# Fewer dummy matmuls ahead of the first transposes and ahead of the first FFN step of a fused attention and SwiGLU kernel

## The chip, the cores and the metric

The kernel runs on one core of a Trainium2 chip. The metric is the device time of one launch in microseconds; it was 333.8 us before the change (median of ten runs).

## What is computed

Sliding-window causal attention (8 batches, 8 heads, 576 positions, head dimension 64, window 64) is followed by a SwiGLU block over the 4608 resulting tokens (512 wide, hidden width 1536). Inputs and output are float32; the kernel works in bfloat16 with float32 accumulation.

```python
scores = scale * np.matmul(q, k.transpose(0, 1, 3, 2))
mask = (rel >= 0) & (rel < window)          # window = 64, rel = query - key
scores = np.where(mask, scores, -1000000000.0)
...                                          # softmax over keys
attn_out = np.matmul(attn, v)
x = attn_out.transpose(0, 2, 1, 3).reshape(B * S, H * D)
g = x @ w_gate
silu = g * (1.0 / (1.0 + np.exp(-g)))
val = x @ w_val
return (silu * val) @ w_out
```

## The kernel before

The tokens are cut into 36 tiles of 128 for the attention, and into 9 chunks of 512 (four tiles each) for the FFN. One list of operations is written down in program order; a small graph class finds from the buffers that each one reads and writes which semaphores it has to wait for, and every engine then runs its own operations in the order of that list. Nothing is reordered later, so the text of the list sets the order on each engine.

The list begins with two strings. `LOADS` issues the loads, nearly all on GpSimd's queue (the first tile's k and q go out on SyncE's and ScalarE's queues as float32, line 291). `STEPS` (from line 166) is the order of the work for tiles 0 to 15 and FFN chunks 0 and 1, by hand, one token for each step; from chunk 2 on a loop in `build` issues the rest. The tokens that matter here:

- `warm:50` (line 348): 50 matmuls of 64 columns over a zeroed tile `wz`, at the very start. `W:n` (`fill`, line 359): n dummy matmuls of 512 columns over `wz`, into the PSUM bank that has been free for longest. Nobody reads what they write. They wait for `wz` alone.
- `B` (line 403): a matmul that writes the mask's bias into a bank ahead of the scores. `ca`, `cd`: the cast of the first tile's q and k to bfloat16, one half on ScalarE (line 300) and one on VectorE (line 302), after their load. `T:0:1`, `T:0:0` (line 310): the transposes of those halves on TensorE; `ea`, `ed` copy the results to `kT` and `qT`.
- `TQ`, `TK` (line 310) transpose q and k of later tiles, and `qa`, `kd` and the like copy them out. `S` (line 423) are the scores with their exponentials (line 433), `M` the mask product (line 439), `A0` and `A1` (line 473) the product with v in two phases, `N` the normalisation on VectorE (lines 492 and 495), which writes `xb`; `X` (line 570) the transposes of `xb`, and `xa`, `xd` their copies to `xT`.
- `F:c:f` (line 604): for FFN chunk c and hidden block f, four matmuls with the gate weights and four with the value weights, then tanh on ScalarE (line 610). `U` (lines 613 and 615): the two VectorE steps that make the hidden block. `O` (line 637): the output projection. `ld`, `wo`: further loads.

So TensorE's order at the start is: 50 small dummies, two `B` matmuls, ten dummies, eight transposes of tile 0, four of q of tile 1, one dummy, the scores of tile 0, and so on, up to the fourth `X` and the first `F`.

Of the kernel before, what the change touches and what calls it, by code (L numbers as in the profile page):

```python
# [7 lines left out]
B, H, S, D = 8, 8, 576, 64  # L8
DM, DFF = H * D, 1536
T = B * S  # L10
# [139 lines left out]
class _Kernel:  # L150
# [13 lines left out]
    w:5:6 v:7 kq:6 w:0:1 kq:7 w:10:12  # L164
    """
    STEPS = """
    warm:50 ld:8 wo:0:6 B:0 ca:0:0 cd:0:1 W:10 T:0:1 T:0:0 ea:0:1 ed:0:0 TQ:1 qa:1 W:1 S:0 TK:1 ld:9 kd:1 W:1
    TQ:2 qa:2 S:1 B:2 TK:2 kd:2 A0:0 A1:0 M:1 S:2 TQ:3 N:0 B:3 TK:3 qa:3 kd:3 W:1 X:0 A0:1 xa:0 S:3 A1:1 ld:10
    A0:2 N:1 A1:2 ld:11 W:1 A0:3 N:2 A1:3 X:1 xa:1 N:3 W:1 X:2 xa:2 W:3 X:3 F:0:7:0:384 xd:3 U F:0:8 U TK:5
    TQ:5 ka:5 TQ:4 F:0:7:384:512 TK:4 ld:12 qa:4 qd:5 ka:4 U W:2 F:0:3 U S:4 S:5 F:0:6 M:4 F:0:4 M:5 U F:0:1 U  # L170
    U A0:4 A0:5 A1:4 ld:13 wo:6:12 A1:5 F:0:9 N:4 N:5 X:4 F:0:2 U xa:4 X:5 U F:0:5 xd:5 F:1:1:0:128 U TQ:6
    F:1:2:0:256 U TK:6 ld:14 qa:6 F:1:3:0:256 U F:0:0 kd:6 U U S:6 TK:7 TQ:7 F:1:0:0:256 kd:7 F:0:10 M:6 U
# [612 lines left out]
```

## Time and profile before

| | before |
|---|---|
| median of ten runs | 333.8 us (333.0 to 334.82) |
| profiled execution | 333.93 us, span 332.1 us |
| TensorE busy | 325.9 us (98%) |
| VectorE, ScalarE, GpSimd busy | 217.0, 137.3, 115.8 us |
| TensorE from 0 to 18.8 us, from 18.8 to 72 us | first FFN matmul at 19.03; 53.14 of 53.20 us busy |
| chain that ended last | TensorE 95%, VectorE 3% |
| `fill` (line 359) on that chain | 1% of the span |

Times in the profile are counted from the start of the span, which is 1.83 us shorter than the execution's own time. Matmuls are pipelined: a row of the timeline with ten matmuls has the length from the start of the first to the end of the last, and the end of a matmul is about 0.16 us after its last column has gone in when the array runs fast. Weight loads (PEld) are rows of their own and run ahead of the matmuls that use them. "[idle before <-releaser]" is the time for which the engine had nothing to run before that row, and what ended it.

### The profile page before, as it was taken

What the parts mean: (1) busy time and instruction counts of PE and PEld (TensorE: products, weight loads), DVE (VectorE), ACT (ScalarE), POOL (GpSimd) and SP (SyncE); (2) the same over time, 40 slices, a digit from 0 to 9 for tenths busy, and PEclk for the clock granted to TensorE, in tenths of its full rate; (3) what the DMA queues carried; (4) which work ended last, traced back from release to release, by engine and by line L of the source; (5) the groups of instructions that cost most, each with busy time, mean ns of one, the idle gap of its engine ahead of it and who ended that gap; (6) DMA issues with size and microseconds to landing.
All of it is one profiled execution on the core that took longest, in us unless ns stands there. A gap on an engine that the chain in (4) does not pass through costs nothing.

```text
span 332.1 us, 8397 instructions
## 1 busy us (share of the span) xinstructions
PE 325.9 (98%) x3552; PEld 166.3 (50%) x3552; DVE 217.0 (65%) x454; ACT 137.3 (41%) x249; POOL 115.8 (35%) x144
## 2 busy tenths in 40 slices
PE   8899999989999999999999999999999999999997
PEld 5555666564454445454545454545454544444444
DVE  6568989993458757676767676767666666555520
ACT  2855466563244525252525253434342522233222
POOL 8999999983008606060706060100000000000000
PEclk9999999999999999999999999999999999999999
DMA  9999999999999999999999999542415111100012
GB/s 132 166 169 170 168 178 156 178 156 173 211 156 126 118 173 74 181 70 185 60 160 98 178 74 156 94 126 34 129 26 134 28 69 29 68 34 32 32 58 103
DMA packets 168837, 38.70 MB, mean 117 GB/s; under 512 B 159328, under 2 KB 164320, under 8 KB 168800
## 3 DMA queue, kind: packets, MB, share of 16 engines
q0 software_dynamic: 122560, 18.62, 83.7%
q1 hardware_dynamic: 45568, 19.21, 28.5%
q8 instruction: 28, 0.46, 0.5%
q10 hardware_dynamic: 672, 0.33, 0.3%
q14 instruction: 9, 0.07, 0.1%
HBM read 37.75 MB, written 9.44 MB: 142 GB/s over the span
## 4 chain that ended last, share of the span: by engine, by line
PE 95%; DVE 3%; issue 1%; ACT 0%
PE ps L604 56%; PE ps L637 28%; PE ps L423 3%; PE ps L536 2%; PE ps L310 1%; PE ps L473 1%; DVE xb L495 1%; PE ps L359 1%; PE ps L667 1%; PE ps L570 1%; PE ps L403 0%; DVE kT L302 0%; DVE rc L492 0%; DVE mask L267 0%; DVE pt L439 0%
## 5 line engine op out<-in xcount | busy, mean ns | idle before, releaser
L613 DVE SCALAR_TENSOR_TENSOR uu<-sig,ps 128x512 bf16<-128x512 bf16 (+3 forms) x116 | 75.2, 649 | 67.2 <-ACT sig L610 67.0
L604 PE MATMUL ps<-xT,Wv 128*128 128x512 bf16 (+3 forms) x464 | 112.4, 364 | 0.9 <-issue 0.9
L604 PE MATMUL ps<-xT,Wg 128*128 128x512 bf16 (+3 forms) x464 | 112.3, 364 | 0.1
L610 ACT ACTIVATE sig<-ps 128x512 bf16<-128x512 f32 (+3 forms) x116 | 65.8, 569 | 87.7 <-PE ps L604 87.6
L637 PE MATMUL ps<-Wo,hT 128*128 128x512 bf16 x420 | 97.8, 379 | 0.0
L615 DVE SCALAR_TENSOR_TENSOR hT<-uu,ps 128x512 bf16<-128x512 bf16 (+3 forms) x116 | 75.4, 650 | 4.0
L373 POOL DMA_DIRECT2D va<-in_v_dram x40 | 40.2, 1030 | 93.0 <-PE ps L536 87.8
L604 PEld LDWEIGHTS ps<-xT,Wv 128*128 128x128 bf16 x464 | 44.7, 98 | 50.1 <-issue 1.1
L604 PEld LDWEIGHTS ps<-xT,Wg 128*128 128x128 bf16 x464 | 43.7, 98 | 46.3 <-issue 0.8
L637 PEld LDWEIGHTS ps<-Wo,hT 128*128 128x128 bf16 x420 | 39.9, 98 | 46.6
L649 ACT ACTIVATE ost<-ps 128x512 f32<-128x512 f32 x35 | 20.9, 598 | 67.2 <-PE ps L637 67.0
L433 ACT ACTIVATE pt<-ps 128x512 bf16<-128x512 f32 x72 | 37.7, 601 | 25.9 <-PE ps L423 25.7
L283 POOL DMA_DIRECT2D qn<-in_q_dram x39 | 39.9, 1042 | 1.4 <-POOLq L770 0.8
L283 POOL DMA_DIRECT2D kn<-in_k_dram x39 | 40.1, 1048 | 0.7 <-DMA kn<-in_k_dram 0.7
L439 DVE TENSOR_TENSOR pt<-pt,mask 128x512 bf16<-128x512 bf16 x66 | 24.3, 419 | 0.3
L558 DVE TENSOR_TENSOR xb<-ps,rp 128x448 bf16<-128x448 f32 (+1 forms) x36 | 18.5, 513 | 1.2
L555 DVE RECIPROCAL rp<-ps 128x7 f32<-128x7 f32 (+1 forms) x36 | 6.7, 187 | 15.5 <-PE ps L536 15.5
L423 PE MATMUL ps<-qT,kT 64*64 64x64 bf16 (+1 forms) x864 | 15.8, 203 | 0.5 <-DVE qT L302 0.4
L423 PEld LDWEIGHTS ps<-qT,kT 64*64 64x64 bf16 x864 | 12.2, 108 | 7.2 <-DVE hT L615 4.2
L536 PE MATMUL ps<-va,pt 64*64 64x65 bf16 x728 | 11.5, 193 | 0.1
L495 DVE TENSOR_TENSOR xb<-ps,rc 128x256 bf16<-128x256 f32 x24 | 10.2, 425 | 0.8
L379 POOL DMA_DIRECT2D Wg<-in_moe_w_gate_dram x10 | 9.8, 976 | 0.0
(51 smaller groups left out, 110.5 us busy)
## 6 DMA issues: line engine op xcount, KB each, us to landing
out_dram<-ost SPq DMA_DIRECT2D x35, 256.0 KB, 3.5
va<-in_v_dram POOLq DMA_DIRECT2D x32, 128.0 KB, 6.5
qn<-in_q_dram POOLq DMA_DIRECT2D x31, 128.0 KB, 7.3
kn<-in_k_dram POOLq DMA_DIRECT2D x31, 128.0 KB, 7.4
Wo<-in_moe_w_out_dram POOLq DMA_DIRECT2D x2, 768.0 KB, 11.5
Wg<-in_moe_w_gate_dram POOLq DMA_DIRECT2D x8, 128.0 KB, 5.2
Wv<-in_moe_w_val_dram POOLq DMA_DIRECT2D x8, 128.0 KB, 5.2
Wg<-in_moe_w_gate_dram POOLq DMA_DIRECT2D x2, 256.0 KB, 5.7
```

The source lines that it names most:

```text
L283: self.g.op("pool", lambda e, d=d, a=a: e.dma_start(d, a), writes=ks, dma=True)
L373: g.op("pool", lambda e, d=d, a=a: e.dma_start(d, a), writes=ks, dma=True)
L423: r = e.matmul(sv[h][o:o + 64, c, q0:q1], self.kT[ps, c, kk:kk + 64], qT[ps, c, q0:q1], start=not biased, stop=not biased or c == 3 and kk ...
L433: g.op("act", lambda e, po=po, si=si: e.activation(po, si, ACTF.Exp, scale=SCALE), reads=[bk], writes=[pk])
L439: "dve", lambda e: e.tensor_tensor(po, po, m, ALU.mult), reads=[pk, "mask"], writes=[pk]))
L558: g.op("dve", lambda e, xo=xo, rb=rb, a=a: e.tensor_tensor(xo, a[:, :, 0:64], rb, ALU.mult), reads=[bk] + rk, writes=wk)
L604: r = e.matmul(bank[:, 0:n], W[:, kk, f * 128:f * 128 + 128], xT[:, kk, t0:t1], start=(kk == 0), stop=(kk == NK - 1))
L610: g.op("act", lambda e: e.activation(sig[:, 0:n], G[:, 0:n], ACTF.Tanh, scale=0.5), reads=[gk], writes=[("sig", i)])
L613: g.op("dve", lambda e: e.scalar_tensor_tensor(uu[:, 0:n], sig[:, 0:n], 1.0, G[:, 0:n], ALU.add, ALU.mult), reads=[("sig", i), gk], writes ...
L615: g.op("dve", lambda e: e.scalar_tensor_tensor(hT[:, f, t0:t1], uu[:, 0:n], 0.5, V[:, 0:n], ALU.mult, ALU.mult), reads=[("uu", i), vk], wr ...
L637: r = e.matmul(OB[:, :], hT[:, f, 128 * u:128 * u + 128], self.Wo[:, f, :], start=(f == 0), stop=(f == NF - 1))
L649: g.op("act", lambda e: e.activation(ost[:, :], OB[:, :], ACTF.Copy), reads=[ok], writes=[("ost", io)])
```

## The change

Two numbers in `STEPS` are changed: four dummies instead of ten ahead of the first transposes (`T:0:1`), and one instead of three ahead of the fourth `X`, which is followed by the first FFN step. On TensorE eight dummy matmuls and their eight weight loads are gone; the instructions of the other engines and all DMAs are the same, in the same order.

```diff
     STEPS = """
-    warm:50 ld:8 wo:0:6 B:0 ca:0:0 cd:0:1 W:10 T:0:1 T:0:0 ea:0:1 ed:0:0 TQ:1 qa:1 W:1 S:0 TK:1 ld:9 kd:1 W:1
+    warm:50 ld:8 wo:0:6 B:0 ca:0:0 cd:0:1 W:4 T:0:1 T:0:0 ea:0:1 ed:0:0 TQ:1 qa:1 W:1 S:0 TK:1 ld:9 kd:1 W:1
...
-    A0:2 N:1 A1:2 ld:11 W:1 A0:3 N:2 A1:3 X:1 xa:1 N:3 W:1 X:2 xa:2 W:3 X:3 F:0:7:0:384 xd:3 U F:0:8 U TK:5
+    A0:2 N:1 A1:2 ld:11 W:1 A0:3 N:2 A1:3 X:1 xa:1 N:3 W:1 X:2 xa:2 W:1 X:3 F:0:7:0:384 xd:3 U F:0:8 U TK:5
```

## The prediction

> **What bounds the kernel now.** I read the page first. Its first part and the by-engine line of its fourth say that TensorE sets the end:
>
> ```profile
> PE 325.9 (98%) x3552; PEld 166.3 (50%) x3552; DVE 217.0 (65%) x454; ACT 137.3 (41%) x249; POOL 115.8 (35%) x144
> PE 95%; DVE 3%; issue 1%; ACT 0%
> ```
>
> Busy TensorE can still be useless TensorE: both edits take away dummies (line 359), which are work that nobody reads. So the question is whether a dummy lies on the chain. The second view is the chain of waits from 3 to 20 us (start, length, what):
>
> ```profile
> 4.33 1.04 PE ps L403 x2
> 5.37 2.61 PE ps L359 x10
> 7.97 0.46 PE ps L310 x8
> 8.46 0.42 DVE kT L302
> ...
> 18.32 0.43 DVE xb L495
> 18.75 0.05 issue
> 18.80 0.40 PE ps L570 x4
> ```
>
> The ten dummies are on the chain, with 2.61 us: the first transposes (L310) start when the last dummy has gone through, not when their data are there. The three dummies ahead of the fourth X (L570 at 18.80) are not on it: that step is released by VectorE's last normalisation (xb, L495). Third, when are the data of the first transposes there? The timeline of ScalarE and VectorE:
>
> ```profile
> 6.22 0.63 ACT L300 ACTIVATE cc<-ff 128x512 bf16<-128x512 f32 x1 [3.23 <-DMA ff<-in_k_dram]
> 6.23 0.67 DVE L302 CAST cc<-ff 128x512 bf16<-128x512 f32 x1 [0.27 <-DMA ff<-in_k_dram]
> ```
>
> The load of k lands, both casts start at once, and the later ends at 6.23 + 0.67 = 6.90. In TensorE's timeline the first transpose starts at 7.81. Fourth, how fast are the dummies? Their weight loads, in the timeline, stand one ahead of each dummy:
>
> ```profile
> 4.74 0.15 PEld L359 LDWEIGHTS ps<-wz 128*128 128x128 bf16 x1 [0.28 <-DVE wz L271]
> 5.16 0.15 PEld L359 LDWEIGHTS ps<-wz 128*128 128x128 bf16 x1 [0.28 <-issue]
> 5.59 0.15 PEld L359 LDWEIGHTS ps<-wz 128*128 128x128 bf16 x1 [0.28 <-issue]
> 6.01 1.46 PEld L359 LDWEIGHTS ps<-wz 128*128 128x128 bf16 x7 [0.28 <-issue]
> ```
>
> The loads come 0.42 to 0.43 us apart up to 6.01; the next seven take 1.46 us together, about 0.22 us apart. TensorE's clock doubled there, near 6.15 us. (The clock column of the stretches shows 1.00 from time zero, so it does not tell of this; the spacing does.) Dummies one to three were slow, and the other seven fast.
>
> Last, the waits of TensorE alone from 20 us to the end, one row:
>
> ```profile
> PE ps L604 <- issue: 0.9, 1, 0.9
> ```
>
> After the fourth X, TensorE waits for nothing else that the profile names. Time saved ahead of it should reach the end.
>
> **Ten dummies to four.** Removed: six loads and six 512-column matmuls. The dummies start at 5.16, 5.59, 6.01 and 6.30 (the third, half slow and half fast, took 0.29). The fifth would start 0.22 later, at 6.52; there TensorE is now free, and has to wait for the cast, 6.90. Not all of the six come back, then: 6 x 0.216 = 1.30 us of dummies, less the idle time 6.52 to about 6.95. The chain shows 0.05 us from the end of a VectorE step to TensorE's start (18.75 to 18.80), so the first transpose goes from 7.81 to 6.95: **0.86 us earlier**. From there the chain is transposes, evictions on ScalarE and VectorE, scores, exponentials, normalisations; every piece hangs on the one before.
>
> What stays fixed in time is the loads, issued by GpSimd in a row whatever TensorE does. I read issue and time to landing of those needed next. q of tile 1: issued 1.25, 5.2 to landing, 6.4; needed at 8.26, now 7.40. k of tile 1: 2.25 + 4.9 = 7.1, needed 9.65, now 8.8. v of tile 0: 4.88 + 4.8 = 9.7, needed 11.70, now 10.84. The closest is v of tile 2: 8.34 + 5.8 = 14.1, needed at about 15.0, now at 14.15. It just holds; if it came 0.2 late, VectorE, which has normalisations queued from 15.36 to 18.75 without a break, would cover it: the output of that attention step is wanted by VectorE at 16.47, and it is done by 15.75. The first FFN weights: 10.82 + 6.4 = 17.2 for the value half, needed 19.5, now 18.7. For the FFN blocks to 45 us, landings and uses are 2 us or more apart. So 0.86 carries to the first FFN step. From there TensorE issues without a wait. Its queue runs ahead of the array (some waits are passed 3 us before the matmul), and GpSimd's and SyncE's queues get no new instruction and no new wait.
>
> **Three dummies to one.** The row that decides is TensorE's load queue at the fourth X:
>
> ```profile
> 18.79 0.23 PEld L570 LDWEIGHTS ps<-ident,xb 128*128 128x128 bf16 x4 [0.54 <-DVE xb L495]
> ```
>
> The three dummies start at 17.93 and the last has gone in at 18.58; X waits until 18.80 for VectorE. Two fewer, 2 x 0.216 = 0.43 us, only lengthen that wait. I cost this at nothing; the cover is VectorE's chain of normalisations. If that cover were gone, the edit would gain up to 0.43 us.
>
> **The sum.** The profiled execution took 333.93 us (span 332.1 and 1.83 around it), 0.13 above the median of 333.80. 333.93 - 0.86 - 0 = 333.07; on the median's scale 332.94. I say 333.0.
>
> **The unknown: the clock.** The dummies also make TensorE look busy, and the clock followed that. In the 3.4 us before it doubled (2.74 to 6.15), the view by stretches has TensorE busy for 2.95 of 3.41 us, 86%; in the stretch ending at 2.74 it was busy only from 1.02, 50%. What lies between is not known. After the rise, stretches of 3.41 us have 3.00, 3.26, 3.01 and 3.18 busy, and the clock stays. With the change, the stretch 6.15 to 9.56 has the fourth dummy to 6.68, then the old contents of 7.81 to 10.42 moved up, of which 8.86 to 9.27 is idle: 0.53 + 2.20 = 2.73, 80%. This is below all that the trace shows as safe, and above what it shows as too little. I take it as safe, being nearer to 88% than to 50%.
>
> The Trainium skill ("TensorE: Matmul & The Clock Gate", Part 1) says that the gate looks at free-running windows of about 3.4 us, that the phase differs from run to run, and that it takes an idle window to lose the full rate. This agrees with the rise at 6.15, after 5.1 us of nearly unbroken work, and by it the change loses nothing after the rise. The same page speaks against the change in Part 4: transposes do not count as busy for the gate. By that, the six dummies are replaced by work that mostly doesn't count, and a run whose window ends late could stay at half rate until the FFN. So by Part 1 the sum stays as it is, and by Part 4 such a run would be the first rival below. No row here shows whether transposes count.
>
> The moment of the rise also bears on the gain, and the trace has one execution of it. Had the clock risen at 4.4, all the dummies would have been fast and the ten would end near the cast: gain about 0. Had it risen at 7.8, it would be (7.8 - 6.15) x 0.49 larger, as each microsecond of slow rate costs half in dummies: 1.7. The ten runs lie 1.8 us apart (333.0 to 334.82), about that width, so the profiled rise near the middle is a fair typical case.
>
> **The rivals.**
> 1. *The clock is lost* (slower). Rows: the 80% above, and the 0.54 us wait at the fourth X, which grows by 0.43. It decides if a stretch that is 80% busy, much of it with 128-column transposes where there were dummies, is too little. For one stretch of 3.4 us, the chain's own TensorE pieces between 9.27 and 12 are 0.45 + 0.34 + 0.45 + 0.54 + 0.24, about 2.0 us, which would double: +2.0 - 0.86, or 335.0. If the clock stays low until the FFN is running: chain pieces of TensorE from 7.97 to 18.8 are about 4 us, and the first 3.4 us of FFN then do half their work (1.7 us): +5.7 - 0.86, 338.7. Against: stretches of 88% hold it with ease.
> 2. *The gain is taken back later* (no change). The 0.9 us in the waits' only row after 20 us is a stop at 72.46 (the next matmul of the same group starts at 73.59) in the middle of a group, with nothing released. If what it waits for comes at a fixed time, TensorE gets there early and stands up to 0.86 longer: 333.1 to 333.9, I say 333.7. Against: in a group there is no new data to wait for, so it may as well move along, or vanish (a gain of up to 1.1 more).
> 3. *The three dummies do bear on it*: 0.43 more gain, 332.5. Against: the row at 18.79.
>
> **Chances.** Forecast (332.5 to 333.4): 0.60. Rival 1: 0.20, half of it brief. Rival 2: 0.13. Rival 3, or the stop vanishing: 0.07. A measurement of this kernel can tell some 0.2%, 0.67 us, so faster means under 333.13: most of the forecast, 0.44, and the 0.07. Slower, over 334.47: rival 1, 0.20. The rest, 0.29, is same. Leaving out the long half of rival 1 and the outer part of the third, the range is 332.4 to 335.0.
>
> **What would show it.** Right: the first transpose at 6.95, the first FFN matmul near 18.2 instead of 19.03, four dummies with the last start at about 6.3, X's wait longer by 0.4, and the last rows of the chain earlier by 0.8. Wrong: transposes at 0.107 instead of 0.056 apart, or 512-column matmuls 0.427 apart after 7 us (clock); a first FFN matmul at 18.2 and an end that has not moved (rival 2); a wait for va on TensorE before 16 us.

## The result

| | before | after |
|---|---|---|
| median | 333.88 us (38 runs, 332.66 to 339.17) | 332.31 us (11 runs, 331.63 to 332.75) |
| ratio | | 0.9953, 95% interval 0.9942 to 0.9963 |
| profiled execution | 333.93 us, span 332.1 us | 332.52 us, span 330.7 us |
| first transpose, first FFN matmul | 7.81, 19.03 us | 6.96, 18.11 us |

The kernel is faster by 1.57 us, or 0.47%. The forecast was 333.0; the measured time lies 0.1 below its range. The early steps came as predicted. In the chain of waits of the kernel after (start, length, what), dummies no longer stand ahead of the first transposes; the load of k and its cast do:

```profile
0.74 5.43 DMA ff<-in_k_dram
...
6.27 0.65 DVE cc L302
6.92 0.05 issue
6.96 0.63 PE ps L310 x8
```

Its timeline of TensorE's weight loads shows the four dummies and what ended the idle time after them. Further down it shows the fourth X, whose wait for VectorE grew from 0.54 to 0.81 us:

```profile
4.72 0.75 PEld L359 LDWEIGHTS ps<-wz 128*128 128x128 bf16 x4 [0.26 <-DVE wz L271]
6.96 0.45 PEld L310 LDWEIGHTS ps<-ident,cc 128*128 128x128 bf16 x8 [1.49 <-DVE cc L302]
...
17.87 0.23 PEld L570 LDWEIGHTS ps<-ident,xb 128*128 128x128 bf16 x4 [0.81 <-DVE xb L495]
```

The rest of the gain lies far behind. The waits of TensorE from 20 us to the end have one row again, but a smaller one and on another line, the output projection's:

```profile
PE ps L637 <- issue: 0.4, 1, 0.4
```

TensorE stands idle at one place there, called the stop from here on. The weight loads show it best. Before (the last column is idle time ahead of a row, and what ended it):

```profile
72.41 0.10 PEld L604 LDWEIGHTS ps<-xT,Wv 128*128 128x128 bf16 x1
73.59 0.17 PEld L604 LDWEIGHTS ps<-xT,Wv 128*128 128x128 bf16 x3 [1.08 <-issue]
```

After:

```profile
71.76 0.76 PEld L637 LDWEIGHTS ps<-Wo,hT 128*128 128x128 bf16 x5
73.23 2.68 PEld L637 LDWEIGHTS ps<-Wo,hT 128*128 128x128 bf16 x13 [0.71 <-issue]
```

Before, TensorE stops after the first of four loads of a value group. After, it gets through the other three of that group and five loads of the output projection, eight pairs of load and matmul further on in the program, and the stop is shorter. Eight pairs is the number that the change removes near the start: the stop stands at the same count of TensorE's instructions, behind the 1097th recorded weight load in both. The other gaps of the two traces are at the same place in the program.

ScalarE's 249 steps follow TensorE and are the same in all kernels, so their starts, taken against the profile before, show where time was won (us; the columns are places in the program, named by the time that they have before):

| | start of FFN, 21 us | just before the stop, 72 us | after it, 77 us | last step |
|---|---|---|---|---|
| after | -0.93 | -0.93 | -1.41 | -1.45 |

So 0.93 was won at the start and 0.48 at the stop.

### The profile page after: what moved, and what is told of

Read it like the earlier page. It is cut to its first block, busy times and chain, and to the rows that moved or that the text cites. A ratio compares the mean times of both kernels' runs of the same rounds, so it can differ in the third digit from the quotient of the medians.

```text
span 330.7 us, 8381 instructions
## 1 busy us (share of the span) xinstructions
PE 323.4 (98%) x3544; PEld 165.1 (50%) x3544; DVE 217.0 (66%) x454; ACT 137.3 (42%) x249; POOL 115.8 (35%) x144
## 4 chain that ended last, share of the span: by engine, by line
PE 94%; DVE 2%; DMA 2%; issue 0%; ACT 0%; DVEq 0%
PE ps L604 57%; PE ps L637 28%; PE ps L423 3%; PE ps L536 2%; DMA ff<-in_k_dram 2%; PE ps L310 2%; PE ps L473 1%; DVE xb L495 1%; PE ps L667 1%; PE ps L570 1%; DVE kT L302 0%; DVE rc L492 0%; DVE pt L439 0%; DVE cc L302 0%; ACT sig L610 0%
## 5 line engine op out<-in xcount | busy, mean ns | idle before, releaser
L373 POOL DMA_DIRECT2D va<-in_v_dram x40 | 38.9, 998 | 90.7 <-PE ps L536 87.8
L283 POOL DMA_DIRECT2D qn<-in_q_dram x39 | 38.6, 1008 | 2.9 <-issue 2.1
L283 POOL DMA_DIRECT2D kn<-in_k_dram x39 | 38.8, 1014 | 0.2 <-issue 0.2
```

What stands on the lines that cost most here:

```text
L283: self.g.op("pool", lambda e, d=d, a=a: e.dma_start(d, a), writes=ks, dma=True)
L373: g.op("pool", lambda e, d=d, a=a: e.dma_start(d, a), writes=ks, dma=True)
```

## The experiments

Theory A: the dummies' instructions, not only their time, matter; a stop at a fixed count of TensorE's instructions moved to a place where it costs less. Theory B: the two dummies ahead of the fourth X were worth something after all. In the table further down "instructions" is the count of TensorE's instructions against the kernel before (after: 16 fewer).

**e1_first_only** has the first edit alone.

```diff
-    ... cd:0:1 W:10 T:0:1 ...
+    ... cd:0:1 W:4 T:0:1 ...
```

> Four dummies ahead of the first transposes, three kept ahead of the fourth X. Theory A (a stop of TensorE at a fixed count of its instructions, near matmul 1097, took the rest of the gain): first transpose at 6.96, first FFN matmul about 0.85 earlier than before, and the stop still after about matmul 1097 of TensorE, now inside the output projection, 0.4 to 0.9 us long; in all 1.0 to 1.5 us less than before. Theory B (the two dummies ahead of the fourth X are worth the missing 0.6 us): 0.85 less than before, no more.

Measured: 332.39 us, ratio 0.9968 (0.9956 to 0.9980). First FFN matmul 18.13. The stop, in its weight loads:

```profile
71.77 0.33 PEld L637 LDWEIGHTS ps<-Wo,hT 128*128 128x128 bf16 x3
72.97 3.12 PEld L637 LDWEIGHTS ps<-Wo,hT 128*128 128x128 bf16 x15 [0.87 <-issue]
```

Six pairs fewer, and the stop is six further on (three of the value group, three here). The first edit carries nearly the whole gain: 1.42 us of 1.57 in the medians.

**e2_second_only** has the second edit alone.

```diff
-    ... xa:2 W:3 X:3 ...
+    ... xa:2 W:1 X:3 ...
```

> Ten dummies kept ahead of the first transposes, one ahead of the fourth X. Theory A: the start of the first FFN matmul unchanged (19.03), four instructions fewer on TensorE, so the stop lies two matmuls of 128 columns further on: 0 to 0.3 us less than before. Theory B: about 0.6 us less than before, and the first FFN matmul earlier by as much.

Measured: 333.56 us, ratio 1.0006 (0.9991 to 1.0022): no difference that can be told. Its profiled execution is a case of an early clock; the ten dummies, in its weight loads, take 1.93 us instead of 2.7, and the fourth X:

```profile
4.67 1.93 PEld L359 LDWEIGHTS ps<-wz 128*128 128x128 bf16 x10 [0.23 <-DVE wz L271]
...
17.94 0.23 PEld L570 LDWEIGHTS ps<-ident,xb 128*128 128x128 bf16 x4 [0.81 <-DVE xb L495]
```

Another profile of the unchanged kernel (e10, below) also has the early clock, and there X starts at 17.93 after a wait of 0.54. With the same start, three dummies or one give the same X, 17.93 and 17.94, and the same first FFN matmul, 18.17 in both. Theory B falls. e2 removes two pairs, and its stop is two pairs further on, still in the value group and 1.08 us long.

**e3_before_16_fewer** leaves all dummies of 512 columns in place, and takes 16 instructions from the very start.

```diff
-            for _ in range(count):
-                r = e.matmul(bank[:, 0:64], self.wz[:, 0:128], self.wz[:, 0:64], start=True, stop=True)
+            for n in [64] * 34 + [128] * 8:
+                r = e.matmul(bank[:, 0:n], self.wz[:, 0:128], self.wz[:, 0:n], start=True, stop=True)
```

> The kernel before, with the 50 warming matmuls of 64 columns at the very start made into 42 (34 of 64 columns and 8 of 128: the same columns in all, 16 instructions fewer, like the change), and all later dummies as before. Theory A: the work up to the first FFN step unmoved (first transpose 7.8, first FFN matmul 19.0 where the clock rises as before), the stop near matmul 1097 five matmuls into the output projection and shorter, 0.4 to 0.7 us instead of 1.08: 0.4 to 0.7 us less than before. Theory B: no difference.

Measured: 333.04 us, ratio 0.9985 (0.9968 to 1.0001); the interval just reaches 1. In the profile the FFN starts 0.05 later than before, and after the stop TensorE is 0.71 ahead. The stop stands where the changed kernel has it, after five loads:

```profile
72.72 0.76 PEld L637 LDWEIGHTS ps<-Wo,hT 128*128 128x128 bf16 x5
73.92 2.04 PEld L637 LDWEIGHTS ps<-Wo,hT 128*128 128x128 bf16 x10 [0.44 <-issue]
```

No dummy of 512 columns was touched, and the stop moved and shrank. The expected 0.4 to 0.7 came out as 0.76 there, and as 0.77 in the medians (333.81 before in the same session).

**e4_after_16_more** and **e6_after_16_more_wide** go the other way: the changed kernel with the instruction count of before. e4 has narrow matmuls among the extra ones, e6 has not.

```diff
-            for _ in range(count):
-                r = e.matmul(bank[:, 0:64], self.wz[:, 0:128], self.wz[:, 0:64], start=True, stop=True)
+            for n in [64] * 42 + [32] * 16:      # e4; in e6: [64] * 58
+                r = e.matmul(bank[:, 0:n], self.wz[:, 0:128], self.wz[:, 0:n], start=True, stop=True)
```

> The changed kernel with the 50 warming matmuls made into 58 (42 of 64 columns and 16 of 32: the same columns, 16 instructions more, so that the count of TensorE's instructions is that of before). Theory A: first transpose at 6.96 as in the changed kernel, the stop back in the FFN group of 128 columns and about 1.1 us long: 0.4 to 0.7 us more than the changed kernel, 0.85 to 1.1 less than before. Theory B: as the changed kernel.

> The changed kernel with 58 warming matmuls of 64 columns in place of 50: the instruction count of the kernel before, with wide matmuls, unlike e4 (which had 16 of 32 columns and measured 333.6). The first 58 end before the first mask matmul at 4.33. If the count alone gave e4 its time: 333.2 to 333.8, with the stop in the FFN group of 128 columns. If e4's narrow matmuls kept the clock low in most runs and so cost part of it: 332.8 to 333.1.

Measured: 333.60 us, ratio 0.9996 (0.9980 to 1.0012), and 333.51 us, ratio 0.9990 (0.9978 to 1.0003). This is more than Theory A allowed: with the count of before, nearly the whole gain of the change is gone, though the FFN starts at 17.95 and 17.85 (in these two executions the first casts also started early, at 5.9 instead of 6.3 us, so that the first transposes stand at 6.40 and 6.44). Narrow matmuls are not the reason, since e6 has none. The stop is back in the value group in both, with 1.21 and 0.91 us in their profiles; but e6's profiled execution (332.63) was the fastest of its twelve. Its stop, in its weight loads:

```profile
71.56 0.10 PEld L604 LDWEIGHTS ps<-xT,Wv 128*128 128x128 bf16 x1
72.58 0.17 PEld L604 LDWEIGHTS ps<-xT,Wv 128*128 128x128 bf16 x3 [0.91 <-issue]
```

So the same kernel was profiled once more, as **e11_same_as_e6**:

> The kernel of e6 for another profile. Its median of 333.5 is 0.9 above its first profiled execution (332.63, stop 0.91 us, first transpose early at 6.44). If the stop is what differs: a stop of 1.5 to 2 us here in an execution of 333.3 to 333.7. If the start differs: a stop of about 1 us, and the first FFN matmul later than 17.85.

It took 333.74 us; first FFN matmul 18.19. The stop, in its weight loads:

```profile
71.83 0.10 PEld L604 LDWEIGHTS ps<-xT,Wv 128*128 128x128 bf16 x1
73.50 0.17 PEld L604 LDWEIGHTS ps<-xT,Wv 128*128 128x128 bf16 x3 [1.58 <-issue]
```

Both differ: the stop is 0.67 longer (1.58 against 0.91 us at the same place), and the first FFN matmul is 0.34 later than in e6 (18.19 against 17.85). ScalarE's starts show two places where time is given back in e11: 0.26 of the 0.84 that the first FFN matmul had gained is lost at a stop of the same kind, on the second FFN group (e6, e4 and e10 lose 0.25 to 0.26 there too; the changed kernel and e5 lose nothing), and 0.49 at the stop near 72 us.

**e10_before_again** and **e12_after_again** are further profiles of the two kernels.

> The kernel before, for another profile of it: first transpose at 6.96 to 8.6 as the clock rises at 4.4 to 7.8, and the stop in the FFN group of 128 columns after the same load of weights. If the stop ends at a time of its own (rival 2), a late start has a shorter stop and an early one a longer; if its length goes with the count alone, it is 1.08 to 1.2 us again.

> The changed kernel, for another profile: the clock up anywhere from 4.4 to 7.8, the first transpose at 6.3 to 7.0 whichever it is, the first FFN matmul at 17.8 to 18.2, the stop after five loads of the first output projection and 0.4 to 0.8 us long, 332.0 to 332.6.

e10 took 333.12 us: the clock up at 3.81, the first transpose at 6.96, the stop 0.93. With an early start its stop is not longer, so its end is not simply fixed in time; nor is its length the 1.08 to 1.2 that the count alone would give. e12 took 331.92 us, just under the expected range: first transpose 6.95, first FFN matmul 18.05, stop 0.40 after five loads. It moved 0.99 ahead by the FFN's start and a further 0.80 at the stop, where the first profile has 0.93 and 0.48.

**e5_after_16_fewer** and **e8_after_32_fewer** go on beyond the change.

```diff
-            for _ in range(count):
-                r = e.matmul(bank[:, 0:64], self.wz[:, 0:128], self.wz[:, 0:64], start=True, stop=True)
+            for n in [64] * 34 + [128] * 8:      # e5; in e8: [64] * 18 + [128] * 16
+                r = e.matmul(bank[:, 0:n], self.wz[:, 0:128], self.wz[:, 0:n], start=True, stop=True)
```

> The changed kernel with the 50 warming matmuls made into 42 (34 of 64 columns and 8 of 128; the same columns, 16 instructions fewer than the changed kernel). Theory A (the stop near 72 us is tied to the count of TensorE's instructions): it moves eight matmuls on, past the first output projection, where TensorE arrives 1.5 us or more later, and shrinks to 0 to 0.3 us: 0.3 to 0.6 us less than the changed kernel, 331.7 to 332.0. If what the stop waits for also comes later by as much as TensorE does, it stays at 0.5 us and the time at 332.3. The count makes no difference: 332.3.

> The changed kernel with the warming matmuls made into 34 (18 of 64 columns and 16 of 128; the same columns, 32 instructions fewer than the changed kernel). Theory A: the stop moves 16 matmuls on from where the changed kernel has it, and TensorE arrives 3 us or more later: no stop, 331.6 to 331.9, like e5 or a little less. The count makes no difference: 332.3.

e5: 331.91 us, ratio 0.9942 (0.9930 to 0.9955). The whole output projection and the one after it go through; the stop is gone:

```profile
71.67 4.86 PEld L637 LDWEIGHTS ps<-Wo,hT 128*128 128x128 bf16 x24
```

e8: 332.96 us, ratio 0.9970 (0.9958 to 0.9982), slower than e5 and a miss for Theory A as it was put. It has nothing near 72 us, but between 45 and 60 us it gives back 1.34 us, in stops that the kernel before does not have there, the larger ahead of an FFN group:

```profile
56.33 0.21 PEld L473 LDWEIGHTS ps<-va,pt 64*64 64x64 bf16 x16
57.38 0.55 PEld L604 LDWEIGHTS ps<-xT,Wg 128*128 128x128 bf16 x4 [0.84 <-issue]
```

Where the count puts the stops is what matters; fewer instructions are not better by themselves. Taken apart in the medians, the count alone (e3) is worth 0.77 us, the dummies' time alone (e4, e6) 0.21 and 0.29, with intervals that reach 1 in all three, and both together 1.57.

| | instructions | dummies first / fourth X | median, us | FFN start against before | gained at the 72 us stop |
|---|---|---|---|---|---|
| e3 | 16 fewer | 10 / 3 | 333.04 | +0.05 | 0.76 |
| e4, e6 | same | 4 / 1 | 333.60, 333.51 | -0.83, -0.92 | -0.12, 0.17 |
| after | 16 fewer | 4 / 1 | 332.31 | -0.93 | 0.48 |
| e5 | 32 fewer | 4 / 1 | 331.91 | -1.01 | 1.07 |
| e8 | 48 fewer | 4 / 1 | 332.96 | -1.21 | 1.07, after 1.34 lost |

(The last two columns are from ScalarE's starts in one profile each; "FFN start" is the second FFN group, 21.39 us before, behind the 0.26 of e4 and e6.)

**e7_little_warming** tests the first rival, the lost clock: 53 warming matmuls of 8 columns and one dummy, with the instruction count of the changed kernel.

```diff
-            for _ in range(count):
-                r = e.matmul(bank[:, 0:64], self.wz[:, 0:128], self.wz[:, 0:64], start=True, stop=True)
+            for n in [8] * 53:
+                r = e.matmul(bank[:, 0:n], self.wz[:, 0:128], self.wz[:, 0:n], start=True, stop=True)
...
-    ... cd:0:1 W:4 T:0:1 ...
+    ... cd:0:1 W:1 T:0:1 ...
```

> The changed kernel with its 50 warming matmuls of 64 columns made into 53 of 8 columns and one dummy in place of four ahead of the first transposes (the instruction count is that of the changed kernel; TensorE is much less busy in the first 6 us). Rival 1 of the prediction (the clock is lost or late when TensorE works little): transposes 0.107 us apart instead of 0.056, the clock up one or more stretches of 3.4 us later, 334 to 339. If the clock follows the scores and transposes alone just as well: up by 9.8 at the latest, 332.3 to 333.0.

Measured: 333.30 us (332.06 to 334.25), ratio 0.9983 (0.9972 to 0.9993), 1.0 more than the changed kernel. Its profiled execution is the slowest of its runs, 334.25. The clock rose only at 12.92, and the eight first transposes take 1.03 us instead of 0.62 (TensorE's timeline):

```profile
6.95 1.03 PE L310 MATMUL ps<-ident,cc 128*128 128x128 bf16 x8 [1.59 <-DVE cc L302]
```

The first FFN matmul starts at 20.01, 1.90 later than after. In the stretches ahead of the rise TensorE was busy for 2.55 and 3.42 us:

```profile
6.09:9.50 3.41, 2.55 (x39) 1.90 (x40) 1.56 (x3) 1.78 (x4) 3.41 (x5) 1.00 2.41 154
9.50:12.92 3.42, 3.42 (x48) 2.14 (x51) 0.47 (x2) 2.77 (x5) 3.42 (x5) 1.00 2.41 157
```

75%, about half of it transposes, did not raise it, though 80% (e1, 2.73 of 3.41 us from 2.93 to 6.34) and 86% (before) did. Whether the share or the transposes made the difference, these runs don't tell. In the changed kernel the stretch after the rise (4.70 to 8.11) has 2.32 of 3.41 busy, 68%, and the clock stayed up. The rival's mechanism is real, and in this slowest execution it costs what was priced (2.0 for a stretch; 1.0 in the medians), but the change does not bring it about.

**e9_no_late_pair** is the version that follows: the changed kernel without the two dummies in front of `F:0:3`, where TensorE waits for nothing, and with the count of e5.

```diff
-            for _ in range(count):
-                r = e.matmul(bank[:, 0:64], self.wz[:, 0:128], self.wz[:, 0:64], start=True, stop=True)
+            for n in [64] * 38 + [128] * 6:
+                r = e.matmul(bank[:, 0:n], self.wz[:, 0:128], self.wz[:, 0:n], start=True, stop=True)
...
-    ... ka:4 U W:2 F:0:3 ...
+    ... ka:4 U F:0:3 ...
```

> The changed kernel without the two dummies of 512 columns that stand ahead of F:0:3 at 22.5 us, where TensorE waits for nothing (two fewer), and with the warming matmuls made into 44 (38 of 64 columns and 6 of 128), so that the instruction count is that of e5 (16 fewer than the changed kernel). If dummies cost their own time where TensorE is the bound: 2 x 0.216 = 0.43 us less than e5, 331.5, with no stop near 72 us, and the fastest of all. If the weights' landing or an eviction stands behind those dummies: 331.9, as e5.

Measured: 331.26 us (330.83 to 331.98), ratio 0.9919 (0.9888 to 0.9949), the fastest of all. The FFN group follows the transposes at once, where e5 has the two dummies between:

```profile
22.13 0.27 PEld L310 LDWEIGHTS ps<-ident,kn 128*128 128x128 bf16 x4
22.36 0.58 PEld L604 LDWEIGHTS ps<-xT,Wg 128*128 128x128 bf16 x4
```

By ScalarE's starts it gains 0.43 there (0.99 to 1.42 ahead), which is 2 x 0.216, and it has no stop near 72 us.

## Why the prediction was right and where it was wrong

- *The chain through the ten dummies*: right. The first transpose moved from 7.81 to 6.96, where 6.95 was computed; the FFN started 0.92 earlier, against 0.86.
- *What stays fixed in time*: right. No load held TensorE up in the changed kernel's profile.
- *The three dummies at nothing*: right; X's wait took their place, and e2 and e10 agree to 0.01 us. In the load queue that wait grew by 0.27 (0.54 to 0.81), not by the 0.4 that was forecast.
- *The clock in the sum*: right that it is safe, and right that the moment of its rise sets what the ten dummies cost: with a rise at 4.35 (e2) and 3.81 (e10) ten dummies end in time and the first transpose starts at 6.96 with them too. So the 0.86 was not as typical as it was taken to be: of the four profiles with ten dummies, two have the first transpose late (7.81 in the profile before, 7.86 in e3) and two (e2, e10) at 6.96, where the first edit would win nothing there. That the profiled execution was a late one is luck. The two kinds of execution also fit the spread of after, 1.1 us against 2.2 before (without the one run of 339.17).
- *The stop at 72.46, a term put at nothing*: this is the step that failed. It was costed as something that stays, takes back the gain (the second rival) or vanishes (part of 0.07), and so the eight removed pairs were costed for their time alone. It stands at a count of TensorE's instructions, and so it moved by the eight pairs, to 512-column matmuls, and became shorter: 0.48 and 0.80 us more were gained there in two profiles. 333.93 - 0.93 - 0.48 = 332.52, which is the profiled time.
- *The second rival* holds in part, for another kernel. With an early start and the old count, the medians are 333.60 and 333.51 (e4, e6): most of the 0.9 is given back, at the second FFN group and at the stop. The dummies' time alone would hardly have shown.

That the stop moves with the count is shown (e1, e2, e3 and e5, and back again in e4 and e6). That it is a wait for instructions was not tested by changing it alone, but the traces leave little room for another cause. No semaphore is waited for there. The instruction queue's 28 packets of 16 KB are about 64 bytes for each of TensorE's 7,200 instructions, so 256 instructions in a packet. Counted as two for each weight load and one for each semaphore wait of TensorE in the trace, the stops stand at 705 (the second FFN group in e4, e6, e10 and e11), 1473 and 1729 (e8) and 2241 (near 72 us, in eleven of the fourteen profiles), within 1 or 2: they are 768, 256 and 512 apart, whole packets. In these eleven profiles the queue's eighth packet ends 1.2 to 1.9 us before TensorE goes on. In the other three TensorE comes to that place 2.6 (e5), 3.1 (e9) and 4.3 us (e8) after the end of that packet, and does not stop.

This also tells why the stop is longer in e11 than in e6: there the eighth packet ends 0.88 us later (72.08 against 71.20), and TensorE goes on 0.92 later. Why a packet comes early in one execution and late in another stays open, and with it how much of the 1.2 us between the medians of e6 and the changed kernel belongs to which stop.

## What to carry to other kernels

A dummy or a wait that is taken out ahead of a dense stretch is worth the time to the next thing that is really late, here the cast of a load; read it off the chain and not off the dummies' sum. An edit that changes the number of an engine's instructions also shifts every later stop that sits at an instruction count, so an "issue" row without a cause belongs into the sum with bounds on both sides. Look at what the instruction queue brought just before it, and run a test at equal count to tell the two effects apart. Dummies inside a stretch where the engine waits for nothing cost their full time, as the pair in e9 did (0.43 us).

## What the runs showed of the hardware

- TensorE stopped for 0.4 to 1.6 us at a fixed place of its instruction stream (2241 instructions by the trace), and went on 1.2 to 1.9 us after the end of a 16 KB packet of the instruction queue; the other stops tied to the count lie whole multiples of 256 instructions away. 32 instructions fewer (before to e5) removed the stop near 72 us; 48 fewer (e8) brought two others, 16 and 24 us earlier.
- The clock rose between 3.81 (e10) and 6.34 us (e1) where the trace records it and the warming was full, with the first matmul at 1.02 in all. In e11 it rose later still, at about 6.8 by an estimate: its fourth dummy, started at 6.44, took 0.56 us, where slow ones took 0.61 and fast ones 0.38. With little warming (e7) it rose at 12.92.
- Once up, the clock stayed up through a stretch of 3.41 us that was 68% busy; a stretch that was 75% busy, about half of it with transposes, did not raise it, and one of 80% did.
